# Block-sparse attention and a token mix on one core: the products of weights and values in another order

## The chip, the core and the metric

The kernel runs on one core of a Trainium2 chip. The metric is the device time of one execution in microseconds, as the median of several runs. TensorE (PE in the profile, its weight loads PEld) multiplies; VectorE (DVE), ScalarE (ACT) and GpSimd (POOL) work element by element; SyncE (SP) issues most transfers, GpSimd the gathers. SBUF is the on-chip memory of 128 partitions, PSUM the memory that TensorE writes its sums to. A product takes a stationary operand (the weights of the array, up to 128 columns) and a moving operand that is streamed past it; the columns of the stationary operand become the partitions of the result. A product of 32 columns can lie in one of four column groups of the array, one of 64 columns in one of two halves. Every product of f32 operands appears in the trace as two passes, each with its own weight load.

## The reference

Attention with a mask of blocks of 32 positions, and then a mix over tokens and channels of its output, in float32:

```python
# q, k, v: 4 batches x 8 heads x 768 positions x 64; sampled_blocks: 24 x 3
scores = scale * np.matmul(q, k.transpose(0, 1, 3, 2))
mask = np.abs(blk_i - blk_j) <= 1
mask = mask | (blk_i == 0) | (blk_j == 0) | (blk_i == n_blocks - 1) | (blk_j == n_blocks - 1)
for qb in range(n_blocks):
    for kb in sampled_blocks[qb]:
        mask[qb * block:(qb + 1) * block, kb * block:(kb + 1) * block] = True
scores = np.where(mask, scores, -1000000000.0)
attn = np.exp(scores - np.max(scores, axis=-1, keepdims=True))
attn = attn / (np.sum(attn, axis=-1, keepdims=True) + 1e-09)
attn_out = np.matmul(attn, v)

x = attn_out.transpose(0, 2, 1, 3).reshape(4, 768, 512)
theta = x @ w_theta
zr, zi = x * np.cos(theta), x * np.sin(theta)
y = np.einsum('ts,bsd->btd', w_tok_r, zr) + np.einsum('ts,bsd->btd', w_tok_i, zi)
u = x + y
out = u + np.maximum(u @ w_ch, 0.0)
```

So a query block sees the first and the last block, its own and its two neighbours, and up to three sampled ones; the first and the last query block see all 24.

## The kernel before

**Tiling.** The four batches are worked on as two halves of two batches (`bp`). Within a half, a head is named by `b` (batch of the half, 0 or 1), `e` (0 or 1) and `p` (0 to 3): 16 heads. The 22 inner query blocks of a half (`i` = 1 to 22) are units of the loop; two that follow each other (an odd one and the next even one) form a pair that shares its common keys. The two edge blocks, which see every key, are done in four wide units ahead of the inner ones (`scores_wide`, `weights_wide`, `turn_wide`, `values_wide`).

**One inner unit.** GpSimd copies the unit's key blocks together (`gather_k`, line 243) and starts a gather of value rows from memory into one of four tiles `vb` (`gather_v`, line 265). TensorE makes the scores of 16 heads into S (line 282): 64 rows, 32 columns, 256 moving elements a product, on four column groups and two row groups. VectorE takes the minimum (line 285), ScalarE the exponential into P (line 294). TensorE turns P by eight transposes into T (line 300), and ScalarE copies T to `pT` (line 302). `pT` exists once; its columns hold, for each head, 32 columns of the odd block (`u` = 0) beside 32 of the even one (`u` = 1).

**The products of a pair** (`values`, line 335). For each of the 16 heads there are three products into the head's 65 columns of X (64 values and the sum of the weights): one with the gathered values of the odd block (`vb`, 32 weight columns), one with those of the even block (another `vb`, 32 weight columns), and one with the values common to both (`va`, 64 weight columns), which adds to the first two. The head's place on the partitions of X is `64 * (p % 2)`, so the vb products of an even `p` lie in column groups 0 and 1, those of an odd `p` in groups 2 and 3; X has one bank of PSUM for each `b`. The order is written out by hand: batch by batch, in each `e` and `p`, with the three products of a head together.

```python
order = [(b, e, p) for b in range(2) for e in range(2) for p in range(4)]
for b, e, p in order:
    for u in range(2):
        weigh(b, e, p, 1, u, 1, vbs[(i - 1 + u) % VB_BUFS], True, False)
    weigh(b, e, p, 0, 0, 2, va, False, True)
```

VectorE then divides by the sums (`normalised`, lines 315 to 319: `sm`, then `xo`), and SyncE stores `xo` to `xs` in device memory (line 348). X, `xo`, T and `pT` have one buffer each, S has two.

**Wide products** (`values_wide`, line 392): for each of two heads (`c`), six products of 64 weight columns that add up into the same 65 columns of X, in column half `c`; first all six of one head, then all six of the other.

**What sets the order.** Attention is recorded under `tc.manual_schedule()`: each engine takes its instructions in the order of the code. In the loop over units, the iteration of an odd block `i` issues the scores of the next unit, then the products of the pair before (`values(bp, i - 2)`), then the exponentials of the next unit and the turning of its own; the iteration of the even block issues scores, turning and exponentials. So TensorE's row of a pair is: products, turn, scores, turn, scores. Between these, VectorE and ScalarE take apart the weights of the second half into two float32r words each (`Decoder`; lines 63 to 84), a fixed share in every unit, and SyncE's queue holds, in order, stores of `xo`, loads of `va`, queries and raw weights. The keys of the second half (`kb`, 3 MB, line 222) go into the only buffer of the first half's, so their load begins when the first half's last scores are made. The token mix (`token_mix`, lines 515 to 700) follows; there a scheduler that works with simulated times sets the order of each engine.

Of the kernel before, what the change touches and what calls it, by code (L numbers as in the profile page):

```python
# [24 lines left out]
VB_BUFS = 4  # L25
# [144 lines left out]
def attention(tc, qT, qE, kT, vr, sampled, xs, ident, pieces, follow):  # L170
# [9 lines left out]
    with ExitStack() as ctx, ExitStack() as early:  # L180
# [23 lines left out]
        vbs = [cp.tile([P, 1040], F32, name=f"vb{x}") for x in range(VB_BUFS)]  # L204
# [117 lines left out]
        def sums_tile(name):  # L322
            return ps_x.tile([P, 2, 512], F32, tag="X", name=f"X{name}")[:, :, 0:260].rearrange("r b (g f) -> r b g f", f=65)
# [3 lines left out]
        def values(bp, i):  # L327
            x = st[bp, i]["X"] = sums_tile(f"{bp}_{i}")
            va = vas[((i - 1) // 2) % VA_BUFS]
            order = [(b, e, p) for b in range(2) for e in range(2) for p in range(4)]  # L330

            def weigh(b, e, p, c, u0, n, v, start, stop):
                r0 = 64 * (p % 2) + 32 * u0
                v0 = 65 * (8 * b + 4 * (p // 2) + 2 * e + p % 2)
                nc.tensor.matmul(  # L335
                    x[r0 : r0 + 32 * n, b, 2 * (p // 2) + e, :], pT_pair[:, 4 * c + 2 * e + b, p, u0 : u0 + n, :], v[:, v0 : v0 + 65],
                    start=start, stop=stop,
                )

            for b, e, p in order:  # L340
                for u in range(2):
                    weigh(b, e, p, 1, u, 1, vbs[(i - 1 + u) % VB_BUFS], True, False)
                weigh(b, e, p, 0, 0, 2, va, False, True)

        def finish(bp, i):
            xo = normalised(f"{bp}_{i}", st.pop((bp, i))["X"], 8)
# [38 lines left out]
        def values_wide(bp, b, pp, e):  # L385
            if (b, pp, e) == (0, 0, 0):
                xws[bp] = sums_tile(f"w{bp}")
            x, v = xws[bp], vws[bp, b, pp]
            for c in range(2):
                for k in range(6):  # L390
                    v0 = 130 * e + 65 * c
                    nc.tensor.matmul(
                        x[64 * c : 64 * c + 64, b, 2 * pp + e, :], pT_wide[:, e, k, 64 * c : 64 * c + 64], v[:, k, v0 : v0 + 65],
                        start=k == 0, stop=k == 5,
                    )
# [36 lines left out]
        with tc.manual_schedule():  # L432
# [14 lines left out]
            for n in range(len(units) + 1):  # L447
# [20 lines left out]
                if is_wide(n):  # L468
                    bp, _, x = units[n]
                    if n and not is_wide(n - 1):  # L470
                        last = units[n - 2][:2]
                        values(*last)
                    turn_wide(bp, *x, 0)
                    if n and is_wide(n - 1):
                        values_wide(bp, *units[n - 1][2], 1)
# [7 lines left out]
                    if n and is_wide(n - 1):  # L483
                        finish_wide(bp, *units[n - 1][2])
                    values_wide(bp, *x, 0)
                elif n == len(units):
                    last = units[n - 2][:2]
                    values(*last)
                    finish(*last)
                else:  # L490
                    bp, i, _ = units[n]
                    if i == 1:
                        values_wide(bp, *units[n - 1][2], 1)
                    elif i % 2:
                        last = bp, i - 2
                        values(*last)
                    if i % 2:
                        do(n + 1, weights, weights_wide)
                        turn(bp, i)
                    else:  # L500
                        turn(bp, i)
                        do(n + 1, weights, weights_wide)
                    decoder.go(phases)
                    if last:
                        finish(*last)
                    if i == 1:
                        finish_wide(bp, *units[n - 1][2])
# [275 lines left out]
```

## Time and profile before

| | us |
|---|---|
| time, median of 3 runs | 726.09 (721.34 to 729.16) |
| the profiled execution | 730.01 |
| its span, first to last instruction | 728.2 |
| attention, until the last products end | 0 to 373 |
| token mix | 373 to 728 |

The mean granted TensorE clock of the span is 0.962 of full speed. Within the span three stretches are told apart below: the pairs of the first half (47.9 to 168), the passage with the second half's wide units (168 to 231), and the pairs of the second half (231 to 373). "Busy" is the time in which an engine has an instruction under way, so a busy TensorE is not yet one whose array is full: passes in different column groups overlap, and the end of a pass is modelled by the profile. In a row of the timeline, a count such as x96 groups neighbouring instructions of one kind; its length runs from the first start to the last end. The chain of waits follows the work that ended last back to the start; an engine's idle time matters only where it stands on that chain.

### The profile page before, as it was taken

How to read it: one execution, taken by the hardware profiler on the slowest of the kernel's cores; microseconds unless marked ns; L12 is line 12 of the kernel's file. 1: busy time of each engine (PE TensorE's matmuls, PEld its weight loads, DVE VectorE, ACT ScalarE, POOL GpSimd, SP SyncE). 2: the span in 40 equal slices, each digit the busy share in tenths (PEclk: the TensorE clock that was granted, in tenths of full speed). 3: DMA queues.
4: the chain of work that ended last, by engine and by line, in shares of the span. 5: the costliest groups of instructions: out<-in, count | busy, mean ns of one | idle time of the engine just before them, and what ended most of it. 6: DMA issues, size and time to landing. Idle time of an engine off the chain costs nothing.

```text
span 728.2 us, 16678 instructions
## 1 busy us (share of the span) xinstructions
PE 681.6 (94%) x6592; PEld 566.3 (78%) x6592; DVE 462.2 (63%) x1063; ACT 333.8 (46%) x708; POOL 133.5 (18%) x262
## 2 busy tenths in 40 slices
PE   5899999997979999999785999999999999999997
PEld 2666666664666666666574999999999999999997
DVE  3676667563268575766427887875668575855753
ACT  3454545453155354535334556543554355633530
POOL 1435444432204444534000000000000000000000
PEclk9999999997589999999898999999999999999999
DMA  8665655866256564654324432242113311121102
GB/s 312 216 206 171 193 192 176 268 187 241 70 178 207 159 198 155 204 189 143 106 63 142 110 95 57 81 125 65 54 42 113 102 62 57 43 77 62 41 0 87
DMA packets 71110, 95.57 MB, mean 131 GB/s; under 512 B 5240, under 2 KB 52984, under 8 KB 71032
## 3 DMA queue, kind: packets, MB, share of 16 engines
q1 hardware_dynamic: 64696, 71.08, 30.9%
q0 software_dynamic: 6336, 23.43, 10.3%
q8 instruction: 52, 0.85, 0.5%
q14 instruction: 26, 0.21, 0.1%
HBM read 81.90 MB, written 12.58 MB: 130 GB/s over the span
## 4 chain that ended last, share of the span: by engine, by line
PE 69%; DMA 12%; DVE 10%; ACT 5%; SPq 2%; issue 2%; DVEq 0%; ACTq 0%
PE X L335 22%; PE y L622 7%; PE y L623 7%; PE y L624 7%; PE T L300 5%; DMA xs<-xo 3%; PE S L282 3%; DMA out_dram<-of 3%; PE SW L365 3%; ACT pT L302 3%; PE h L586 2%; PE h L584 2%; PE h L585 2%; DMA kb<-in_kT_dram 2%; PE o L645 2%; PE o L646 2%
## 5 line engine op out<-in xcount | busy, mean ns | idle before, releaser
L335 PE MATMUL X<-va,pT 128*64 128x65 f32 x704 | 118.4, 251 | 0.0
L335 PE MATMUL X<-vb,pT 128*32 128x65 f32 x1408 | 114.3, 236 | 1.5 <-ACT pT L302 1.1
L243 POOL COPY kg<-kb 128x256 f32 (+2 forms) x202 | 88.2, 477 | 67.8 <-PE S L282 33.8
L335 PEld LDWEIGHTS X<-va,pT 128*64 128x64 f32 x704 | 68.8, 138 | 34.2 <-issue 2.8
L302 ACT COPY pT<-T 128x1024 f32<-128x1024 f32 x44 | 44.6, 1014 | 96.7 <-PE T L300 96.5
L294 ACT ACTIVATE P<-S,m 128x256 f32<-128x256 f32 x176 | 69.1, 479 | 39.6 <-DVE m L285 39.6
L335 PEld LDWEIGHTS X<-vb,pT 128*32 128x32 f32 x1408 | 54.1, 109 | 35.3 <-ACT pT L302 1.3
L285 DVE TENSOR_REDUCE m<-S 128x2 f32<-128x512 f32 x88 | 56.4, 682 | 24.6 <-PE S L282 24.5
L265 POOL DMA_INDIRECT vb<-in_vr_dram,rows x44 | 43.3, 985 | 140.4 <-PE X L335 133.6
L622 PE MATMUL y<-w_tok_r_hi,zh 128*128 128x384 f32 x192 | 65.1, 339 | 2.8 <-DVE xo L319 1.6
L584 PE MATMUL h<-w_theta_hi,xTh 128*128 128x256 f32 x192 | 57.2, 298 | 10.5 <-ACT xTh L575 10.5
L623 PE MATMUL y<-w_tok_r_lo,zh 128*128 128x384 f32 x192 | 64.4, 335 | 0.0
L624 PE MATMUL y<-w_tok_r_hi,zl 128*128 128x384 f32 x192 | 64.2, 335 | 0.0
L623 PE MATMUL y<-w_tok_i_lo,zh 128*128 128x384 f32 x192 | 64.2, 334 | 0.0
L622 PE MATMUL y<-w_tok_i_hi,zh 128*128 128x384 f32 x192 | 64.2, 334 | 0.0
L624 PE MATMUL y<-w_tok_i_hi,zl 128*128 128x384 f32 x192 | 61.3, 334 | 0.0
L586 PE MATMUL h<-w_theta_hi,xTl 128*128 128x256 f32 x192 | 56.8, 297 | 1.4 <-DVE xTl L576 1.4
L585 PE MATMUL h<-w_theta_lo,xTh 128*128 128x256 f32 x192 | 56.4, 294 | 0.0
L300 PE MATMUL T<-ident,P 128*128 128x128 f32 x352 | 49.0, 283 | 4.0 <-ACT pT L302 1.6
L300 PEld LDWEIGHTS T<-ident,P 128*128 128x128 f32 x352 | 38.6, 143 | 15.9 <-ACT pT L302 13.7
L282 PE MATMUL S<-kg,q 64*32 64x256 f32 x1408 | 48.9, 387 | 0.0
L315 DVE TENSOR_SCALAR sm<-X 128x8 f32<-128x8 f32 x22 | 3.6, 165 | 70.1 <-PE X L335 70.1
(127 smaller groups left out, 1354.6 us busy)
## 6 DMA issues: line engine op xcount, KB each, us to landing
xa<-xs SPq DMA_DIRECT2D x192, 64.0 KB
vw<-in_vr_dram SPq DMA_DIRECT2D x8, 780.0 KB
kb<-in_kT_dram SPq DMA_DIRECT2D x8, 768.0 KB
xr<-xs SPq DMA_DIRECT2D x96, 64.0 KB
out_dram<-of SPq DMA_DIRECT2D x32, 192.0 KB
va<-in_vr_dram SPq DMA_DIRECT2D x22, 260.0 KB
q<-in_qT_dram SPq DMA_DIRECT2D x22, 256.0 KB
xs<-xo SPq DMA_DIRECT2D x44, 128.0 KB
```

The costliest lines, as they stand in the source:

```text
L243: nc.gpsimd.tensor_copy(dst, blocks.rearrange("r g s f -> r s g f"))
L282: nc.tensor.matmul(sc[32 * p : 32 * p + 32, e, b, :], q[rows, b, p, :], keys[rows, :, :, 4 * b + p, :], start=True, stop=True)
L294: nc.scalar.activation(pt[:, e, b, :], sc[:, e, b, :], AF.Exp, bias=m[:, e, b : b + 1], scale=-1.0)
L300: nc.tensor.transpose(t[:, k, :], pt, ident)
L302: nc.scalar.copy(out, t.rearrange("r k (p q) -> r k p q", p=4) if len(out.shape) == 4 else t)
L335: nc.tensor.matmul(x[r0 : r0 + 32 * n, b, 2 * (p // 2) + e, :], pT_pair[:, 4 * c + 2 * e + b, p, u0 : u0 + n, :], v[:, v0 : v0 + 65], star ...
L584: nc.tensor.matmul(ps, hi[:, c, :], wh[:, c, :], start=c == 0, stop=False)
L585: nc.tensor.matmul(ps, hi[:, c, :], wl[:, c, :], start=False, stop=False)
L586: nc.tensor.matmul(ps, lo[:, c, :], wh[:, c, :], start=False, stop=c == 3)
L622: nc.tensor.matmul(acc, zh[:, dd], wh[:, j, tt], start=j == 0 and m == 0, stop=False)
L623: nc.tensor.matmul(acc, zh[:, dd], wl[:, j, tt], start=False, stop=False)
L624: nc.tensor.matmul(acc, zl[:, dd], wh[:, j, tt], start=False, stop=j == 5 and m == 1)
```

## The change

In `values`, the list of heads is gone. For each `e` and each pair of `p` (`pp`), four heads are taken together: both batches `b`, and `p` = 2 pp and 2 pp + 1. First come their eight products with `vb`, which lie in column groups 0, 1, 2, 3 for the first batch and then in 0, 1, 2, 3 for the second; then their four products with `va`, in the two halves for the first batch and then for the second. In `values_wide`, the loops over `k` and `c` change places, so that the two column halves take turns. Number, shape and operands of all products stay the same.

```diff
-            order = [(b, e, p) for b in range(2) for e in range(2) for p in range(4)]
-
             def weigh(b, e, p, c, u0, n, v, start, stop):
...
-            for b, e, p in order:
-                for u in range(2):
-                    weigh(b, e, p, 1, u, 1, vbs[(i - 1 + u) % VB_BUFS], True, False)
-                weigh(b, e, p, 0, 0, 2, va, False, True)
+            for e in range(2):
+                for pp in range(2):
+                    heads = [(b, e, 2 * pp + c) for b in range(2) for c in range(2)]
+                    for head in heads:
+                        for u in range(2):
+                            weigh(*head, 1, u, 1, vbs[(i - 1 + u) % VB_BUFS], True, False)
+                    for head in heads:
+                        weigh(*head, 0, 0, 2, va, False, True)
...
-            for c in range(2):
-                for k in range(6):
+            for k in range(6):
+                for c in range(2):
                     v0 = 130 * e + 65 * c
                     nc.tensor.matmul(
```

Two lines are added in all, so lines behind them have numbers higher by two in the changed kernel (the products are line 333 there, the wide ones 394).

In the built program, attention's instructions stand in the same order on every engine apart from these products. In the token mix the scheduler sets another order in places, from the end of attention on.

## The prediction

> **What bounds the kernel now.** I read the page's busy shares and its chain first, then the chain in order of time, then windows over the steady stretch, and last TensorE's timeline inside one window of products. The page:
>
> ```profile
> PE 681.6 (94%) x6592; PEld 566.3 (78%) x6592; DVE 462.2 (63%) x1063; ACT 333.8 (46%) x708; POOL 133.5 (18%) x262
> ...
> PE 69%; DMA 12%; DVE 10%; ACT 5%; SPq 2%; issue 2%; DVEq 0%; ACTq 0%
> ```
>
> TensorE carries most of the chain. In order of time (start, length, what), one pair of query blocks reads:
>
> ```profile
> 243.91 8.15 PE X L335 x96
> 252.06 1.04 PE T L300 x8
> 253.18 1.02 ACT pT L302
> 254.24 1.09 PE T L300 x8
> 255.33 1.02 PE S L282 x32
> 256.36 8.15 PE X L335 x96
> ```
>
> A pair takes 256.36 - 243.91 = 12.45 us: 8.15 in the products that the change reorders (48 products, two passes each) and 4.30 in turning, copying and scores. Two windows (length, then busy us of PE, PEld, DVE, ACT, POOL, the clock, DMA share, GB/s):
>
> ```profile
> 231.52:331.02 99.50, 98.43 (x1410) 65.44 (x1410) 65.62 (x109) 47.59 (x95) 45.54 (x85) 1.00 0.59 186
> 122.53:147.79 25.26, 24.62 (x353) 16.29 (x353) 15.28 (x26) 11.87 (x24) 12.46 (x25) 1.00 0.80 257
> ```
>
> The first holds eight pairs of 12.44 us: TensorE is busy 99% of it, VectorE 65.62 / 8 = 8.2 us a pair, GpSimd 5.7, ScalarE 5.9, and the queues move 186 GB/s. TensorE alone sets the pace, and it is the only engine that does.
>
> **The change, part by part.** Where a product's pass goes in the array can be read from TensorE's timeline, cut so that a row ends after so many passes (start, length to the end of the last pass, count); the two rows with three durations are minimum, median and maximum of one pass:
>
> ```profile
> 244.54 0.25 PE L335 MATMUL X<-vb,pT 128*32 128x65 f32 x2
> 244.54 0.31 PE L335 MATMUL X<-vb,pT 128*32 128x65 f32 x4
> 244.78 0.33 PE L335 MATMUL X<-va,pT 128*64 128x65 f32 x2
> 245.04 0.31 PE L335 MATMUL X<-vb,pT 128*32 128x65 f32 x4
> 240.57 0.45 PE L282 MATMUL S<-kg,q 64*32 64x256 f32 x8
> 240.57 0.88 PE L282 MATMUL S<-kg,q 64*32 64x256 f32 x24
> 206.45 0.62 PE L392 MATMUL Xw<-vw,pT 128*64 128x65 f32 x7
> 206.45 0.68 PE L392 MATMUL Xw<-vw,pT 128*64 128x65 f32 x8
> L335 PE MATMUL X<-vb,pT x1408: 217/244/318, 47.8 to 372.6; 128*32 128x65 f32 x176
> L392 PE MATMUL Xw<-vw,pT x384: 222/222/370, 17.0 to 226.5; 128*64 128x65 f32 x192
> ```
>
> Four prices follow. (a) One more pass on the same columns: 0.68 - 0.62 = 0.06 us. The first step also shows its weight load: 0.68 - 0.22 - 6 x 0.06 = 0.10 to 0.11 us for 64 columns. (b) Passes on different column groups overlap: two passes of 0.24 us end 0.25 us after the first began, so they start 0.01 apart; the next two come 0.08 later. (c) Four column groups overlap as well: the scores put eight passes (four column groups by two row groups) into one round, and two more rounds add 0.88 - 0.45 = 0.43, so 0.21 a round. (d) A change of the weights' shape costs a gap: the last pass on vb starts at 244.54 + 0.31 - 0.22 = 244.63, the next one, on va, at 244.78: 0.15 us where a repeated pass costs 0.06.
>
> So a head costs 0.24 (vb) + 0.26 (va) = 0.50 us today, 0.15 us twice of it the shape change; 16 heads are 8.0 us, and some 0.15 is the start. TensorE's order before, at the first products of a pair (X is the output, vb the two gathered tiles, va the common one):
>
> ```order
> L282 MATMUL S0_4_649<-kg_116,q0_3_142 32x256 x16
> L335 MATMUL X0_1_669<-vb0_120,pT_117 32x65
> L335 MATMUL X0_1_669<-vb1_121,pT_117 32x65
> L335 MATMUL X0_1_669<-va0_118,pT_117 64x65
> L335 MATMUL X0_1_669<-vb0_120,pT_117 32x65
> L335 MATMUL X0_1_669<-vb1_121,pT_117 32x65
> ```
>
> and now, at the same place:
>
> ```order
> L282 MATMUL S0_4_649<-kg_116,q0_3_142 32x256 x16
> L333 MATMUL X0_1_669<-vb0_120,pT_117 32x65
> L333 MATMUL X0_1_669<-vb1_121,pT_117 32x65
> L333 MATMUL X0_1_669<-vb0_120,pT_117 32x65
> L333 MATMUL X0_1_669<-vb1_121,pT_117 32x65
> L333 MATMUL X0_1_669<-vb0_120,pT_117 32x65
> L333 MATMUL X0_1_669<-vb1_121,pT_117 32x65
> L333 MATMUL X0_1_669<-vb0_120,pT_117 32x65
> L333 MATMUL X0_1_669<-vb1_121,pT_117 32x65
> L333 MATMUL X0_1_669<-va0_118,pT_117 64x65 x4
> ```
>
> Eight vb products stand together, on the four column groups twice, then four va products on two halves twice: 8 shape changes a pair instead of 32. A block of four heads: vb 0.08 + 0.06 + 0.06, 0.02 for four staggered starts, 0.15 for the shape change = 0.37; va 0.11 + 0.06 + 0.06 + 0.01 + 0.15 = 0.39. Four blocks and the start: 4 x 0.76 + 0.15 = 3.2 us instead of 8.15, 4.95 less. Its bounds: 2.5 (the eight shape changes cost no more than a repeated pass, 0.06) and 6.6 (passes overlap only as far as in rival C).
>
> The wide products (L392) keep number and operands and alternate column halves: 0.11 + 10 x 0.06 + 0.01 + 0.15 = 0.87 us instead of the 1.37 below, 0.5 less where TensorE is waited for. Nothing else of attention is moved: the other engines' instructions and transfers there stand as before. Two of them wait for the products' end and are released sooner: the gathers on GpSimd's queue, which refill vb, and VectorE's normalising, which frees X.
>
> **What is late next.** TensorE would need 4.30 + 3.2 = 7.5 us a pair, below VectorE's 8.2. That 8.2 holds stretched instructions and is followed by waits (the two L77 rows: this window, and one from 47.92 to 122.53; mean ns after the bar, last the idle time before):
>
> ```profile
> L285 DVE TENSOR_REDUCE m<-S 128x2 f32<-128x512 f32 x32 | 20.5, 682 | 7.9 <-PE S L282 7.9
> ...
> L77 DVE SCALAR_TENSOR_TENSOR raw_tok_i<-raw_tok_i,ds_tok_i 128x512 f32<-128x512 uint32 x3 | 4.7, 1574 | 0.1
> ...
> L77 DVE SCALAR_TENSOR_TENSOR raw_tok_i<-raw_tok_i,ds_tok_i 128x512 f32<-128x512 uint32 x1 | 0.7, 693 | 0.0
> ```
>
> The idle time before the reductions is 7.9 / 8 = 1.0 us a pair, so VectorE gives 8.2 to 9.2. The queues carry 186 x 12.44 = 2.31 MB a pair, which at the 257 GB/s of the second window is 9.0 us. I take a period of 9.0 us; ends 7.5 (TensorE alone) and 10.4 (9.2 and as much stretching again, 1.2). Saving: 3.4 us a pair, not 4.95. GpSimd, 5.7 us, stays hidden.
>
> Not every pair is steady. The chain, and a window at the passage from the first half of the batches to the second:
>
> ```profile
> 132.44 14.48 DMA xs<-xo
> ...
> 160.56 11.77 DMA kb<-in_kT_dram
> ...
> 182.99 12.34 PE X L335 x96
> 195.33 1.49 PE Tw L300 x6
> ...
> 199.29 2.42 PE Xw L392 x24
> ...
> 203.54 0.81 PE Tw L300 x6
> 204.35 1.37 PE Xw L392 x24
> ```
>
> First half: nine periods from 47.9 to 160.1, 9 x 3.4 = 31, less 5, since the 14.48 us store would now outlast a period: 26. The products at 160 hide behind the 11.77 us load, which starts only when the last scores are done: 0. Passage: the products at 182.99 run at half clock, 12.34 against about 3.2 x 2.42/1.37 = 5.7; VectorE waits there too, so 4 of 6.6, and 2 for wide products. Second half: eight periods, 27.5, then twice the products themselves, 5 each, since the transfers between the last pairs and the first angles stay as they are: 37.5. Start-up 1. Sum 26 + 6 + 37.5 + 1 = 70; 17 periods (nine and eight) are in it. The token mix keeps its instructions, but the scheduler orders them anew, and I take 0 (8 either way). One place touches attention, TensorE after T1_21: before
>
> ```order
> L584 MATMUL h1_4478<-w_theta_hi_74,xTh0_0_4438 128x256
> L585 MATMUL h1_4478<-w_theta_lo_75,xTh0_0_4438 128x256
> L586 MATMUL h1_4478<-w_theta_hi_74,xTl0_0_4439 128x256
> L300 MATMUL T1_22_4330<-ident_58,P1_22_4304 128x128 x8
> L335 MATMUL X1_21_4342<-vb0_120,pT_117 32x65
> ```
>
> and now
>
> ```order
> L588 MATMUL h0_4454<-w_theta_hi_74,xTl0_0_4439 128x256
> L300 MATMUL T1_22_4330<-ident_58,P1_22_4304 128x128 x8
> L333 MATMUL X1_21_4342<-vb0_120,pT_117 32x65
> L586 MATMUL h1_4478<-w_theta_hi_74,xTh0_0_4438 128x256
> L587 MATMUL h1_4478<-w_theta_lo_75,xTh0_0_4438 128x256
> ```
>
> The last turning no longer stands behind the second set of angles; a us or two, inside those 8. The profiled execution took 730.01 us (span 728.2), 4 above the median of 726.09: 730 - 70 - 3 = 657 us.
>
> **Rivals.** A, TensorE stays the bound: period 7.5, 17 x 1.5 = 26 us less, 631. For it: VectorE's stretched rows may not recur; against: 8.2 us busy. B, transfers bind: loads and gathers need 11 us a pair (2.31 MB at 210 GB/s), 17 x 2 = 34 more, 691. For it: the 14.48 us store; against: 257 GB/s was reached. C, a group's second pass holds up the next group, so that groups overlap only in neighbours: vb 8 x 0.08 + 0.15, va 4 x (0.11 + 0.06) + 0.15, four blocks and the start 6.6, period 10.9, 17 x 1.9 = 32 more, 689. Against it: eight score passes start together. The Trainium skill, "TensorE: Matmul & The Clock Gate", section on packing small matmuls, says that matmuls start and end strictly in program order; by that rule, with both passes of a product in a row, C would be the result. The trace does not bear it out: the second pass of the scores' first group did not hold back the other seven. D, no change: the 0.15 us gap is not the shape's, 726. Against: it stands at every change and at no repetition. E, slower, by the clock:
>
> ```profile
> 172.46 3.05 PE L365 MATMUL SW<-kb,qe 64*64 64x512 f32 x16 [3.12 <-DMA kb<-in_kT_dram]
> ...
> 169.40:182.30 12.90, 7.88 (x37) 4.23 (x40) 6.03 (x8) 5.32 (x7) 3.77 (x6) 0.59 0.48 183
> ```
>
> Around an idle time of 3.12 us the granted clock falls to a mean of 0.59, and the products at 182.99 still run at half. If TensorE's new idle time brought the half clock to the pairs: products 5.7, turning and scores 4.1 x 1.49/0.81 = 7.5, with a wait 13.4 against 12.44; over all 17 pairs that is 16 us more than before, about 740. It decides from some 78% of the time at half clock, where 9.0 to 13.4 crosses 12.44. Against it: the new idle time is a us and a half a pair, in two gaps.
>
> **How the numbers follow.** Forecast 0.62 (its own range 640 to 676: period 8.2 to 10, token mix 8), A 0.13, B 0.13, C 0.05, D 0.03, E 0.04. Range 628 to 692: it takes in A, B and C, and leaves out D, E and the tails. A measurement here tells about 1% from no change: faster 0.93, same 0.03, slower 0.04.
>
> **What would show it.** Right: one L335 window of about 3.2 us; rows "vb x16" and "va x8" in turn; DVE and DMA on the chain between; a wide set of 0.87 us. Wrong: products above 4.5 us (C), L335 windows 12 us apart (B, D), granted clock below 0.9 between 48 and 160 us (E), or a token mix off by more than 8 us.

## The result and the profile after

The changed kernel takes 685.89 us (median of 4 runs, 681.48 to 688.24); the kernel before takes 724.68 us on the same chip. The ratio is 0.9454, with a 95% interval from 0.938 to 0.9528. The profiled execution of the changed kernel took 681.48 us, its span is 679.7 us: 48.5 us less than the 728.2 before, where the prediction's sum was 70 (by the medians the gain is 39, since the profiled execution before was one of the longer ones and this one is the shortest).

The page of the changed kernel, busy shares and chain:

```profile
PE 576.1 (85%) x6592; PEld 501.7 (74%) x6592; DVE 448.6 (66%) x1063; ACT 334.9 (49%) x708; POOL 140.6 (21%) x262
...
PE 48%; DMA 34%; DVE 10%; SPq 3%; ACT 3%; issue 2%; DVEq 0%; ACTq 0%
DMA xs<-xo 26%; PE y L624 9%; PE y L625 9%; PE y L626 9%; PE h L588 3%; PE h L586 3%; PE h L587 3%; PE o L647 3%; PE o L648 3%; PE o L649 3%; PE SW L367 3%; DMA kb<-in_kT_dram 2%; DVE xo L319 2%; SPq L350 2%; DMA va<-in_vr_dram 1%
```

TensorE is busy some 105 us less, and the time fell by less than half of that. Transfers went from 12% of the chain to 34%, and one transfer alone, the store of `xo`, holds 26%.

The reordered products themselves, in TensorE's timeline of the changed kernel (start, length, count of passes), from the first of them to the turning that follows:

```profile
54.27 0.64 PE L333 MATMUL X<-vb,pT 128*32 128x65 f32 x16
54.84 0.45 PE L333 MATMUL X<-va,pT 128*64 128x65 f32 x8
55.22 0.43 PE L333 MATMUL X<-vb,pT 128*32 128x65 f32 x16
55.59 0.45 PE L333 MATMUL X<-va,pT 128*64 128x65 f32 x8
55.97 0.43 PE L333 MATMUL X<-vb,pT 128*32 128x65 f32 x16
...
57.08 0.45 PE L333 MATMUL X<-va,pT 128*64 128x65 f32 x8
57.46 0.44 PE L300 MATMUL T<-ident,P 128*128 128x128 f32 x2
```

From 54.27 to 57.46 are 3.19 us where there were 8.15. The first row holds the start, some 0.2 us longer than its like; a block of four heads (vb, then va) takes 55.97 - 55.22 = 0.75 us.

But the pairs do not come 5 us sooner. Windows over the nine periods of each half, from the first products to the tenth (length, then busy us of PE, PEld, DVE, ACT, POOL, the clock, DMA share, GB/s):

```profile
46.99:146.03 99.04, 76.42 (x1593) 53.66 (x1585) 62.75 (x118) 52.79 (x103) 52.21 (x94) 0.84 0.70 221
...
203.58:299.65 96.07, 73.97 (x1592) 51.46 (x1584) 62.94 (x119) 53.63 (x106) 54.30 (x95) 0.91 0.67 214
```

That is 11.0 and 10.7 us a pair. No engine is busy more than 78% of such a window, and the transfers' mean share is 0.70 or less: by these columns nothing is full. The chain in order of time says what the pace is:

```profile
209.09 0.70 DVE xo L319
...
209.81 0.51 SPq L350
210.32 0.05 issue
210.37 11.36 DMA xs<-xo
...
221.85 0.70 DVE xo L319
...
222.57 0.51 SPq L350
...
223.13 8.86 DMA xs<-xo
...
232.11 0.70 DVE xo L319
...
233.40 12.16 DMA xs<-xo
```

One `xo` is written, its store is issued and lands 8 to 12 us later in the second half, and only then may the next `xo` be written, because it has one buffer. X has one buffer too, so the next products wait for that `xo`. The group of L319 in the page of the changed kernel (busy, mean ns, then idle time before it and what ended it), and below it the view by that line of the kernel before (us, times):

```profile
L319 DVE TENSOR_TENSOR xo<-X,sm 128x512 f32<-128x512 f32 x22 | 15.2, 692 | 64.9 <-DMA xs<-xo 62.7
```

```profile
  DMA xs<-xo: 5.8, 3
```

VectorE waited 3 times for a store before, 5.8 us in all; now 17 times, 62.7 us.

### The profile page after: what moved, and what is told of

It reads as the page before. It is cut to its first block, busy times and chain, and to the rows that moved or that the text cites. A ratio compares the mean times of both kernels' runs of the same rounds, so it can differ in the third digit from the quotient of the medians.

```text
span 679.7 us, 16671 instructions
## 1 busy us (share of the span) xinstructions
PE 576.1 (85%) x6592; PEld 501.7 (74%) x6592; DVE 448.6 (66%) x1063; ACT 334.9 (49%) x708; POOL 140.6 (21%) x262
## 3 DMA queue, kind: packets, MB, share of 16 engines
q0 software_dynamic: 6336, 23.43, 10.6%
## 4 chain that ended last, share of the span: by engine, by line
PE 48%; DMA 34%; DVE 10%; SPq 3%; ACT 3%; issue 2%; DVEq 0%; ACTq 0%
DMA xs<-xo 26%; PE y L624 9%; PE y L625 9%; PE y L626 9%; PE h L588 3%; PE h L586 3%; PE h L587 3%; PE o L647 3%; PE o L648 3%; PE o L649 3%; PE SW L367 3%; DMA kb<-in_kT_dram 2%; DVE xo L319 2%; SPq L350 2%; DMA va<-in_vr_dram 1%
## 5 line engine op out<-in xcount | busy, mean ns | idle before, releaser
L243 POOL COPY kg<-kb 128x256 f32 (+2 forms) x202 | 94.9, 510 | 62.2 <-PE S L282 25.7
L300 PE MATMUL T<-ident,P 128*128 128x128 f32 x352 | 56.3, 312 | 19.9 <-ACT pT L302 19.4
L300 PEld LDWEIGHTS T<-ident,P 128*128 128x128 f32 x352 | 45.1, 160 | 31.9 <-ACT pT L302 28.9
L333 PE MATMUL X<-vb,pT 128*32 128x65 f32 x1408 | 45.0, 244 | 24.9 <-DVE xo L319 24.8
L333 PEld LDWEIGHTS X<-vb,pT 128*32 128x32 f32 x1408 | 28.5, 119 | 42.0 <-DVE xo L319 32.0
L319 DVE TENSOR_TENSOR xo<-X,sm 128x512 f32<-128x512 f32 x22 | 15.2, 692 | 64.9 <-DMA xs<-xo 62.7
L282 PE MATMUL S<-kg,q 64*32 64x256 f32 x1408 | 53.0, 410 | 3.3 <-DVE q L217 2.0
L586 PEld LDWEIGHTS h<-w_theta_hi,xTh 128*128 128x128 f32 x192 | 38.3, 199 | 16.1 <-ACT P L294 11.9
L333 PE MATMUL X<-va,pT 128*64 128x65 f32 x704 | 44.6, 255 | 0.7 <-DMA va<-in_vr_dram 0.6
```

What stands on the lines that cost most here:

```text
L243: nc.gpsimd.tensor_copy(dst, blocks.rearrange("r g s f -> r s g f"))
L282: nc.tensor.matmul(sc[32 * p : 32 * p + 32, e, b, :], q[rows, b, p, :], keys[rows, :, :, 4 * b + p, :], start=True, stop=True)
L300: nc.tensor.transpose(t[:, k, :], pt, ident)
L333: nc.tensor.matmul(x[r0 : r0 + 32 * n, b, 2 * (p // 2) + e, :], pT_pair[:, 4 * c + 2 * e + b, p, u0 : u0 + n, :], v[:, v0 : v0 + 65], star ...
L586: nc.tensor.matmul(ps, hi[:, c, :], wh[:, c, :], start=c == 0, stop=False)
```

## The experiments

Two theories were tested first. Theory 1: `xo`'s single buffer makes each store's latency a part of the period. Rival 2: the transfers' amount is the limit. Theory 3 came out of the traces of the first four experiments: the store goes to two of the sixteen DMA engines.

**A second buffer of `xo`, in the changed kernel and in the kernel before.** Room for it came from the queries' third buffer.

```diff
-Q_BUFS = 3
+Q_BUFS = 2
-            xo = wp.tile([P, 8, 64], F32, tag="xo", name=f"xo{name}", bufs=1)[:, 0:n]
+            xo = wp.tile([P, 8, 64], F32, tag="xo", name=f"xo{name}", bufs=2)[:, 0:n]
```

> The changed kernel with two buffers of xo instead of one, and two of the queries instead of three to make room for them. Theory 1 (the store of xo sets the pace: with one buffer, the next xo waits until the store before it has landed, and X with it): the idle time of VectorE before L319 put down to that store falls from 62.7 us to under 15, the starts of the products lie about 9.2 us apart in the steady pairs instead of 10.7 (99 us and 96 us for nine periods), and the time falls by 17 x 1.5 = 25 us, to 650 to 668. Rival 2 (the number of bytes sets it: the queues cannot carry a pair in less than 10.7 us): the period stays within 0.4 us, the wait moves to the products, put down to the transfers of va and vb, and the time stays above 678.

Measured: 674.78 us, ratio 0.9292 (0.9226 to 0.9359): some gain, but less than theory 1 asked for, and more than rival 2 allowed, which had the time stay above 678. The wait for the store is gone, and others stand in its place. Waits from 45 to 320 us (total, times, longest), and two rows of the chain:

```profile
DVE q L217 <- DMA q<-in_qT_dram: 41.7, 14, 8.7
...
PEld X L333 <- DMA va<-in_vr_dram: 27.1, 10, 6.6
```

```profile
64.14 14.22 DMA q<-in_qT_dram
...
83.67 14.80 DMA va<-in_vr_dram
```

Loads of some 256 KB land 14 us after their issue. The second buffer was paid for with one of the queries', which could by itself make `q` late; but a later version with the same two buffers of queries and a spread store waits 7.9 us for `q` in all. So the lateness isn't a matter of one buffer: the loads on the queue are late too.

> The kernel before with two buffers of xo and two of the queries. Theory 1: at 12.44 us a pair TensorE hid the store, so the period stays at 12.44 and the time within 1% of before (718 to 731). Rival: the store already cost time before the change, in which case the time falls by more than 1%.

Measured: 728.27 us, ratio 1.0038 (0.9997 to 1.0078): no change. While TensorE set the pace, the store had 12.4 us to land.

**Each half of the change alone.** The products of pairs in the new order with the wide ones in the old, and the other way round.

> Only the new order of the pair products, the wide products as before. Theory 1: all but a few us of the gain, 686 to 693, the wide sets back at 1.37 us. Rival (the wide products at the passage carry a good part): above 697.

Measured: 692.21 us, ratio 0.9543 (0.9473 to 0.9613), as theory 1 said.

> Only the wide products in the new order, the pair products as before. Theory 1: the wide sets take 0.85 us instead of 1.37, but other engines are waited for in those units, so the time is within 1% of before, 715 to 729. Rival: 16 sets x 0.5 us and the half clock around them give 8 us or more, below 715.

Measured: 730.54 us, ratio 1.0051 (1.0017 to 1.0084): no gain, and a little above what was expected. The order of pairs' products is the change; the wide order brings nothing alone, and some 6 us beside it (692.21 against 685.89, which the two intervals do not tell apart). The traces, one each, say where these lie: the wide order takes some 3 us off attention either way (its last products end at 370.1 us against 373.1 in the kernel before, and at 324.9 in the changed kernel against 327.5 with the pairs' order alone), while the token mix behind it takes 359.6 and 359.1 us in the two kernels with half of the change, 355.1 in the kernel before and 354.8 in the changed one. Why the token mix differs is open.

**How far passes overlap, and whether the products still set the pace.** Both kernels keep all products, and only break the blocks of four heads into two. One takes `p` = 2 pp and 2 pp + 1 of one batch (four column groups); the other takes both batches of one `p` (two column groups, each twice):

```diff
+            for b, e, pp in [(b, e, pp) for b in range(2) for e in range(2) for pp in range(2)]:
+                heads = [(b, e, 2 * pp + c) for c in range(2)]
...
+            for e, p in [(e, p) for e in range(2) for p in range(4)]:
+                heads = [(b, e, p) for b in range(2)]
```

> The changed kernel with blocks of two heads instead of four: the two heads of one batch whose products lie in different column groups, four vb products on groups 0, 1, 2, 3 and then two va products on the two halves. 16 shape changes a pair, four groups side by side. Theory (both overlap and shape changes count, by the prices 0.06 a repeated pass, 0.15 a shape change): the products of a pair take 8 x (0.31 + 0.33) + 0.15 = 5.3 us. Rival (only the shape changes count, 0.09 each): 8.15 - 16 x 0.09 = 6.7 us. The time, still held up by the stores, about 690.

> As the one before, 16 shape changes a pair, but the two heads of a block are those of the two batches that lie in the same column groups: four vb products on two groups in turn, then two va products on one half. Theory (overlap counts): 8 x (0.42 + 0.44) + 0.15 = 7.0 us for the products of a pair, 1.7 more than with four groups. Rival (only the shape changes count): the same 6.7 us as with four groups. The time about 705.

Measured: at full clock the products take 4.30 us on four groups and 6.00 us on two (the rows of 96 passes in the chain of each). Both expectations were 1.0 us too high, since they counted a last pass's 0.06 us twice for each shape. Their difference, 1.7 us, is theory's, where the rival said none: passes on different column groups run side by side, and more groups are faster. TensorE's timelines, first on four groups, then on two:

```profile
47.33 0.32 PE L333 MATMUL X<-vb,pT 128*32 128x65 f32 x8
47.58 0.34 PE L333 MATMUL X<-va,pT 128*64 128x65 f32 x4
47.85 0.32 PE L333 MATMUL X<-vb,pT 128*32 128x65 f32 x8
```

```profile
48.57 0.42 PE L333 MATMUL X<-vb,pT 128*32 128x65 f32 x8
48.92 0.45 PE L333 MATMUL X<-va,pT 128*64 128x65 f32 x4
49.30 0.41 PE L333 MATMUL X<-vb,pT 128*32 128x65 f32 x7
```

Two heads take 47.85 - 47.33 = 0.52 us on four groups and 49.30 - 48.57 = 0.73 on two. And the times, one run each, are 693.32 (expected about 690) and 687.62 us (expected about 705): the kernel whose products take 2.8 us a pair more than the changed kernel's is as fast as that one. In the changed kernel the products no longer set the pace. The mean clock of the kernel on two groups is 0.970 where the changed kernel has 0.924, and it is no faster; but in its second half TensorE is busy 91.5 of 94.6 us, so its own work could set its pace there, and it can't say what the half clock costs. Against a cost of the clock in the changed kernel speaks its chain, which in the second half's pairs (203 to 300 us) is 81% stores of `xo`.

**The store in four pieces of 32 rows.** The two stores of a pair copy 2 x 32 rows each, with the pair's two query blocks as the outermost dimension, of size two. Each becomes two stores with 32 rows outermost:

```diff
-                nc.sync.dma_start(xs[bp, i : i + 2, c].rearrange("u q b p f -> u q (b p f)"), xo[64 * c : 64 * c + 64])
+                for u in range(2):
+                    r0 = 64 * c + 32 * u
+                    nc.sync.dma_start(xs[bp, i + u, c].rearrange("q b p f -> q (b p f)"), xo[r0 : r0 + 32])
```

> The changed kernel, one buffer of xo, with each store of xo in four transfers of 32 rows instead of two of 2 x 32 rows. The same bytes. Theory 3 (a transfer of 2 x 32 rows is spread over two of the sixteen DMA engines by its first dimension, so that two engines get 64 packets more a pair than the others, are never idle, and everything queued on them lands late): the time with only two or three DMA engines active goes from a quarter of the steady stretches to under a tenth, the starts of the products come to lie 8.4 to 9.2 us apart instead of 10.7, the idle time of VectorE before L319 falls below 20 us, and the time to 645 to 662. Rival 2 (the bytes of all sixteen set it): the period and the time stay as they were, 680 to 690. Rival 1 (one buffer of xo, with any landing time): the wait before L319 stays above 40 us.

Measured: 629.22 us (625.56 to 633.1), ratio 0.8685 (0.8611 to 0.8759), below what theory 3 expected. Windows over the nine periods of each half, then the page's chain by engine, then stores on the chain in order of time:

```profile
47.91:126.98 79.07, 68.95 (x1593) 48.39 (x1585) 65.70 (x121) 52.30 (x102) 58.16 (x94) 0.96 0.89 275
180.97:253.81 72.84, 66.92 (x1593) 46.65 (x1585) 65.54 (x121) 53.26 (x106) 60.26 (x95) 1.00 0.89 276
```

```profile
PE 54%; DVE 18%; DMA 16%; ACT 4%; SPq 4%; issue 2%; DVEq 0%; ACTq 0%
```

```profile
196.46 5.03 DMA xs<-xo
...
212.58 6.92 DMA xs<-xo
...
237.58 5.80 DMA xs<-xo
```

A pair takes 8.8 and 8.1 us. The queues move the same bytes at 275 GB/s where they moved 214 to 221, stores land in 5 to 7 us in place of 8 to 12, VectorE's wait for them ahead of `xo` falls from 62.7 to 15.1 us, and VectorE is busy 65.54 of 72.84 us, 90%.

> The kernel before with its stores in four transfers of 32 rows. Theory 3: at 12.44 us a pair the two loaded engines kept up and TensorE hid them, so the time stays within 1% of before, 718 to 731, at most a few us less where queries and keys of the second half are loaded. Rival: the stores cost time before the change too, in which case it falls below 715.

Measured: 711.03 us (708.79 to 723.94), ratio 0.9808 (0.9717 to 0.99). The kernel before gains 2%, which the expectation of the rival named (below 715), but not in its steady pairs, which stay at 12.44 us. In its trace the gain lies largely where the chain stood on a late transfer: the 11.77 us load of keys at the passage is off the chain, and the products of the half's last pair run at full clock (7.95 us where they took 12.34):

```profile
148.46 8.15 PE X L335 x96
...
160.90 8.15 PE X L335 x96
...
176.81 7.95 PE X L335 x96
```

**Four pieces cut the other way.** The number of transfers and their size could be what helped, rather than the outermost dimension. Here each of the two stores is cut by batch, so that four stores remain with two outermost:

```diff
+                for b in range(2):
+                    src = xo[64 * c : 64 * c + 64, 256 * b : 256 * b + 256]
+                    nc.sync.dma_start(xs[bp, i : i + 2, c, :, b].rearrange("u q p f -> u q (p f)"), src)
```

> The changed kernel with its store of xo cut into four transfers as well, but the other way: each still has the two query blocks as its outermost dimension (2 x 32 rows x 256 elements, one for each row half and batch), so the number of transfers and their size are those of e7_four_stores. Theory 3 (an outermost dimension of two puts a store on two DMA engines, and these two are what is late): no gain, 676 to 692 us, a pair every 10.5 to 11 us in both halves, the wait ahead of xo still 40 us or more. Rival (four smaller transfers, or their number, are what helped): 626 to 645 us, 8.1 to 9 us a pair, the wait ahead of xo 15 us or so.

Measured: 684.84 us (683.17 to 689.16), ratio 0.9475 (0.9424 to 0.9527): no gain over the changed kernel. The page's group of L319 and the windows:

```profile
L319 DVE TENSOR_TENSOR xo<-X,sm 128x512 f32<-128x512 f32 x22 | 15.2, 691 | 67.6 <-DMA xs<-xo 66.6
```

```profile
47.46:147.61 100.15, 75.54 (x1592) 53.71 (x1584) 61.35 (x119) 53.28 (x105) 52.09 (x94) 0.86 0.70 222
204.84:299.86 95.02, 74.11 (x1593) 51.37 (x1585) 61.18 (x120) 53.66 (x106) 52.40 (x95) 0.89 0.66 214
```

A pair takes 11.1 and 10.6 us. This cut also halves the length of a packet, to 1 KB, but the changed kernel has 2 KB and two outermost, with the same time; of these three only the kernel with 32 rows outermost is at 629. It is that dimension.

**Further along the same line.** The wide units' stores in pieces of 32 rows as well; and, apart from it, the four stores with two buffers of `xo` (and two of the queries).

> e7_four_stores with the stores of the wide units' results cut into transfers of 32 rows too. Theory 3: these stores go to two engines as well, but there are only a few of them, at the start of the pairs and at the passage, so 2 to 6 us less than e7_four_stores: 623 to 629 us. Rival (they lie beside other work): the same as e7_four_stores within its interval, 626 to 633 us.

Measured: 632.25 us, ratio 0.8719 (0.8675 to 0.8762): the same as with the pairs' stores alone. The 2 to 6 us that theory 3 gave these stores did not come; they lie beside other work.

> e7_four_stores with two buffers of xo (and two of the queries in place of three, for room). Theory: with the stores spread, VectorE sets the pace of a pair (66.9 us busy of 72.8 in the second half's nine pairs), and the 15.1 us of waiting ahead of xo are partly cover for it: 0 to 6 us less, 623 to 632 us, the wait ahead of xo gone. Rival (the store still sets the pace): 12 us or more less, 617 us or below.

Measured: 631.37 us, ratio 0.8731 (0.8689 to 0.8773), and no wait for a store is left ahead of `xo`. (The 66.9 us in this expectation are TensorE's; VectorE's are 65.5.) Nor is it faster: with the stores spread, they don't set the pace. The chain of its second half's pairs (176 to 249 us) holds no transfer at all and runs through VectorE, TensorE and ScalarE, though the queues' mean share there is 0.92. The version with four stores and one buffer, at 629.22 us, is the fastest that was run; the other two can't be told from it.

## Why the prediction was right and wrong

The time, 686 us, lies in the range, and the direction is right, but the likeliest case was 657 and its own range ended at 676. That 686 lies in the full range is luck: the range was drawn wide to take in rivals B and C, and neither of these, as it stood, is what happened. (The terms add up to 70.5, and the last step takes off 3 us for the 4 between the profiled execution and the median; neither slip matters here.) By the prediction's steps, measured between the starts of products in the two traces:

| stage | forecast | found |
|---|---|---|
| start-up, to the first products | 1 | 47.85 - 46.99 = 0.9 |
| first half, nine periods | 26 | 112.25 - 99.04 = 13.2 |
| passage, 10th products to the second half's first | 6 | 71.4 - 57.6 = 13.8 |
| second half, eight periods | 27.5 | 99.5 - 85.9 = 13.6 |
| the rest, with the last products | 10 | 7.0 |
| sum | 70 | 48.5 |

**The products, 3.2 us: right** (3.19), and with them the prices of a repeated pass, of overlap and of the change of shape; the kernels with two heads bear out the same prices at 4.30 and 6.00. Rival C, 6.6 us, is refuted. Its ground was a rule of the Trainium skill ("TensorE: Matmul & The Clock Gate", on packing small matmuls), that matmuls start and end strictly in program order; taken as the prediction took it, so that a second pass on a group holds up the next group, the trace disagrees, with 3.19 us; that the order itself was broken isn't shown.

**The wide set, 0.87 us: right.** Chain of the changed kernel, at the passage:

```profile
169.25 3.21 PE X L333 x96
...
175.09 0.85 PE Xw L394 x24
...
180.27 0.85 PE Xw L394 x24
...
189.52 1.02 PE Xw L394 x24
```

**The passage, 6: right in mechanism, too small.** The term supposed that the products there would still run at half clock (5.7 us) and that VectorE would hold back part of the gain. They ran at full clock, 3.21 against 12.34: 9.1 us by themselves, and the units after them gave the other 5. Part of it may belong to the one execution: in the trace of the kernel before with a second buffer of `xo`, which gained nothing, these products ran at full clock too, in 7.99 us.

**The token mix, 0, and the start-up, 1: right.** From the end of the last products the kernel before takes 355.1 us, the changed one 354.8.

**The period of 9.0 us: the step that failed.** It came out at 11.0 and 10.7, which costs the 17 periods some 32 us (9 x 2.0 + 8 x 1.7), of which the term allowed for 5. The step took the queues' 2.31 MB a pair at 257 GB/s, as if sixteen DMA engines were one pipe, and it counted the 14.48 us store once, 5 us, as an odd event. It was the sign of a full resource. The packet records of the traces, counted by how many packets are under way at one time, in windows (us) within the steady pairs, as shares of time; an engine has mostly one under way, so the mean is out of 16:

```
                       none  1 to 3  4 to 12  13 or more  mean
before      50:140     0.06   0.21    0.30      0.44       9.7
before      235:325    0.04   0.25    0.36      0.36       9.0
after       50:140     0.00   0.24    0.22      0.54      10.8
after       205:295    0.00   0.25    0.22      0.53      10.4
four, two outermost
            205:295    0.00   0.28    0.20      0.52      10.3
four of 32 rows
            183:252    0.00   0.03    0.18      0.79      14.0
```

With two engines taking the store, for a quarter of the time one to three packets are under way, and most engines have nothing to do. The records don't name the engine of a packet, but the pages give the number of engines by their count of short packets (nearly all of 4 bytes in the records). The row of the changed kernel, that of four stores with two outermost, and that of four stores of 32 rows:

```profile
DMA packets 71110, 95.57 MB, mean 141 GB/s; under 512 B 5240, under 2 KB 52984, under 8 KB 71032
DMA packets 74014, 95.57 MB, mean 140 GB/s; under 512 B 5328, under 2 KB 58704, under 8 KB 73936
DMA packets 72431, 95.59 MB, mean 151 GB/s; under 512 B 6560, under 2 KB 54304, under 8 KB 72352
```

If every engine that takes part in a transfer ends its share with one short packet, the 88 more of the second row are 4 for each of the 22 pairs: two more stores, on two engines each. The 1320 more of the third row are 60 a pair: four stores on sixteen engines, 64, in place of two stores on two, 4. And with two outermost the four stores, issued together, use the same few engines: between 60 and 140 us only they have packets of 1 KB, and one or two of these are under way for 90% of the time in which any is, never more than four.

That much work on two engines fills a period. A pair's `xo` is 128 rows of 2 KB, 64 for each of two engines; a 2-KB packet takes 84 ns (median in the records), so 5.4 us. The other 2.05 MB of a pair give each of 16 engines 0.128 MB, 31 packets of 4160 bytes at 161 ns, 5.0 us. Together 10.4 us a pair, or 12.7 by the means of the two durations (97 and 209 ns, with what packets wait for each other): an estimate around the 10.7 and 11.0 found. In the kernel before, with 12.44 us a pair, the two just kept up: for 4 to 6% of the time no packet was under way at all, and in the changed kernel that never happens. Spread over sixteen, the store is 8 packets for each engine, 0.7 us, and the whole 5.7 by the medians, or 7.4 by that kernel's means (105 and 212 ns), below its period of 8.1. A load that is spread over all sixteen has a share on the two full engines as well, which explains why the loads ended late with the second buffer.

The Trainium skill, "DMA: Bandwidth & Descriptors", states the rule in the section on why a DMA increments its semaphore by 16: the number of engines is the largest number up to 16 that divides the slowest dimension (of size above one) of both access patterns. By that rule a store with two query blocks outermost has two engines, one with 32 rows has sixteen. The traces agree: the short packets count two engines and sixteen, and the times are 686 and 685 us with two outermost, 629 with 32, the last two with equally many transfers of equal size. The prediction didn't draw on it.

**Rivals A and D are out:** the products fell as forecast, and TensorE is idle for 23% of the pairs' time. **Rival B had nearly the time (691, 11 us a pair) and the wrong reason.** It had the transfers' amount as the limit, at 210 GB/s; the same amount went at 275 GB/s once the store was spread.

**Rival E's sign came, its time didn't.** The prediction named a clock below 0.9 between 48 and 160 us; the first window above shows 0.84. TensorE's timeline of the changed kernel, inside the second window, with idle time and its cause in brackets:

```profile
237.34 1.10 PE L282 MATMUL S<-kg,q 64*32 64x256 f32 x32 [0.29 <-issue]
241.08 1.72 PE L300 MATMUL T<-ident,P 128*128 128x128 f32 x8 [2.64 <-ACT pT L302]
242.72 1.96 PE L282 MATMUL S<-kg,q 64*32 64x256 f32 x32
246.38 0.53 PE L333 MATMUL X<-vb,pT 128*32 128x65 f32 x16 [1.70 <-DVE xo L319]
```

After an idle gap of 2.6 us the turning takes 1.72 us where it took 1.04, the scores 1.96 where they took 1.02, and then TensorE waits 1.70 us for `xo` all the same. So these slow passes, at least, fill time that would be waited out.

**What the forecast of 9.0 was worth.** With the four stores a pair takes 8.8 and 8.1 us, close to VectorE's pace in the prediction (8.2 to 9.2), though VectorE is busy only 65.54 / 9 = 7.3 us of a pair there: the 8.2 were taken from the kernel before, with its stretched instructions. The step named the next engine and missed a resource that no column of busy shares shows as full.

Open is how much of the 629 us could still be had. At 90% VectorE leaves little in the second half's pairs. The first half's 8.8 us hold one period of 13.4 (103.8 to 117.2 us), in which the chain stands on two loads, of 11.05 and 9.33 us; the seven periods before it take 8.0 each.

## What to carry to other kernels

A mean share of the DMA engines of 0.7 doesn't mean room: look at each store's and load's outermost dimension, and take one transfer that lands several times later than its bytes need as a sign to be checked for a few full engines, not as an odd event. When the bound of a kernel is about to fall, ask of every transfer what it would need at the new pace on the engines that it really uses. And where a second buffer removes a wait but others take its place, look for what all of them queue on.

## What the runs showed of the hardware

A store of 2 x 32 rows kept a pair at 10.7 to 11.0 us, the same bytes as 32-row stores at 8.1 to 8.8; in the kernel before, whose pairs hid it, the same cut still gave 2%. The short packets of the traces count two engines for the one and sixteen for the other. Passes in four column groups overlap to 0.75 us for a block of 24 (16 of 32 columns, 8 of 64), start-up aside, which is 0.03 us a pass where one alone takes 0.22.
